# Rest tokens of a fused attention and expert kernel copied out of PSUM at once, and its first microseconds put in another order

## The chip, the cores and the metric

The kernel runs on one core of a Trainium2 chip. The core has a tensor engine (PE, with its weight loads shown as PEld), a vector engine (DVE), a scalar engine (ACT), GpSimd (POOL) and a sync engine (SP), which here only starts transfers. Each engine works through its own list of instructions in order; what one needs of another is told by semaphores. PE writes to PSUM, from which DVE and ACT read; everything else lies in SBUF. The metric is the device time of one execution in microseconds.

## The reference

The inputs are q, k and v of 8 batches, 8 heads, 576 positions and 64 columns, a table of 32 distance buckets by 8 heads, 4608 token numbers, and two weight tables of 8 experts (512x1024 and 1024x512).

```python
scores = (1 / sqrt(64)) * q @ k.T + bias_table[bucket(|i - j|)]
attn   = exp(scores - max) / (sum + 1e-9)
x      = (attn @ v) as 4608 tokens x 512
expert = token_ids * 2654435761 % 8
out[e] = max(x[e] @ w1[e], 0) @ w2[e]      # for each expert's tokens
```

## The kernel before, in words

Attention runs over 32 head pairs: pair n is batch n // 4 and heads 2m and 2m + 1 with m = n % 4. A pair has five score groups g. Groups 0 to 3 take 128 keys each against 512 queries of both heads; group 4 takes what is left over, since 576 is 512 and 64: the 64 "rest" tokens, as keys and as queries. The list `order` names all (n, g) and is worked through two at a time. For each two, PE makes the scores and the bias (products with a table `btb`, or for some groups a factor `ebd` that DVE multiplies in at L550), ACT takes the exponential of a group from PSUM into `att` (L540), then the functions `early` and `behind` add other work: transposes of later pairs, casts, and nine at a time the products of `att` with the values (`px`, L608) of a pair that is some groups back. DVE takes the reciprocal of the sums (L617) and writes the normalised output `x_all` (L618). PSUM has three slots for score groups and two others (aux 0 and aux 1). The output of a pair takes two tiles in turn, one in each of the two.

The order in each engine's list is the order in which the code writes the instructions (`manual_schedule`); nothing is reordered.

Loads: `load(j)` fetches q, k or v of the pairs 2j and 2j + 1 in two DMAs of 256 KB, or half of them with `h0, h1`; `load_rest(b)` fetches the rest tokens of batch b in eight small ones (q, k: L222; v: L234). Nearly all of them are issued by SP, in the order written. An issue takes one of eight semaphores in turn (DMAHW0 to 7 in the rows of the order), and waits until the transfer that used it before has landed. `load(3, "qk")` and `load(2, "v")` are the first ones issued from the loop, right behind the written list of the ramp. `cast_qk`, `cast_v` and `cast_vrest` make 16-bit copies: on POOL, for pairs 4 and up the values on DVE (L254), and for batches 1 and up the upper half of the rest values too (L277).

The bias table is made on the chip: one product (`bps`, L698), a copy by ACT (`ebsb`), a DMA to memory (`t_f`, L706) and from there DMAs that spread it over 128 partitions: `btb` (L712) for heads 0, 1, then 2 and 3, and so on, and the small `btr` (L725).

Rest tokens of a batch, `transpose_rest`: four products turn q and k of the rest tokens round into one PSUM slot (`pr`, L426); three DVE copies take them out, two into `kzr` (L434) and one into `qtr` (L443), and the slot is free after the third. It is called at (m, g) = (3, 0) of the batch before, after the nine `px` products of that step. The rest values go to `vt` in two halves of 64 partitions.

After the last pair the expert stage begins, at about 195 us of the span; it isn't touched.

Of the kernel before, what the change touches and what calls it, by code (L numbers as in the profile page):

```python
# [11 lines left out]
F32 = mybir.dt.float32  # L12
F16 = mybir.dt.float16
# [18 lines left out]
def kernel(  # L32
# [11 lines left out]
    nc = tc.nc  # L44

    B, H, S, D = q.shape
# [6 lines left out]
    P = 128  # L53
# [114 lines left out]
    with tc.tile_pool(name="at", bufs=1) as at, tc.tile_pool(  # L168
# [18 lines left out]
        btb = at.tile([P, H, 3, WB], F16, name="btb")  # L187
        btr = at.tile([P, NPAIR, GL + D + RU], F16, name="btr")
# [9 lines left out]
        qr, kr, vr = {}, {}, {}  # L198
# [17 lines left out]
        def load_rest(b, which="qkv", eng=None):  # L216
            for key, dst, src in (("q", qr, q), ("k", kr, k)):
                if key not in which:
                    continue
                dst[b] = at.tile([P, 2, 2 * D], F32, name=key + "r", bufs=2)  # L220
# [8 lines left out]
            if "v" in which:  # L229
                vr[b] = at.tile([P, NPAIR, D], F32, name="vr", bufs=2)  # L230
                for hh in range(2):
                    for c in range(2):
                        r0 = D * hh + RU * c
                        (eng or nc.sync).dma_start(  # L234
                            out=vr[b][r0 : r0 + RU, :, :],
# [37 lines left out]
        def cast_vrest(b):  # L273
            for hh in range(2):
                r0 = D * hh
                eng = nc.vector if b and hh else nc.gpsimd
                eng.tensor_copy(  # L277
                    out=vt[b % 2][r0 : r0 + D, :, VW * hh : VW * hh + D],
                    in_=vr[b][r0 : r0 + D, :, :],
                )  # L280
# [139 lines left out]
        def transpose_rest(b):  # L420
# [3 lines left out]
            for i, key in enumerate("kq"):  # L424
                for c in range(2):
# [6 lines left out]
                    )  # L432
            for hh in range(2):
# [5 lines left out]
                    in_=pr[D * hh : D * hh + D, 0, :, :].rearrange(  # L439
# [7 lines left out]
                in_=pr[:, 1, :, :].rearrange(  # L447
# [229 lines left out]
        guard.__enter__()  # L677
        load(0, "k", None, 0, 2)
        warm = at.tile([1, 1], F32, name="warm")
        nc.vector.memset(warm[:, :], 0.0)  # L680
        nc.scalar.activation(
# [12 lines left out]
        load(0, "v", None, 0, 2)  # L694

        cast_qk(0, nc.vector, nc.vector)
        bps = slot("bps")
# [24 lines left out]
        for hh in range(2):  # L722
            for c in range(2):
# [7 lines left out]
                )  # L731
        transpose_qk(0)
        for i in range(2):
# [14 lines left out]
        cast_v(0)  # L748
        load(1, "qk")
        load_rest(0, "v")  # L750
        load(0, "v", None, 2)
        load_band(2, 4, nc.sync)
# [6 lines left out]
        load_band(4, 6, nc.sync)  # L759
        load(2, "qk")  # L760
        load_band(6, H, nc.sync)
        load_rest(1)
# [86 lines left out]
        def behind(n, g):  # L849
            G = NIT * n + g  # L850
            b, m = pairs[n]
            if 5 <= n < 11 and g % 2 == 0:
                next(routing, None)
# [8 lines left out]
            if (m, g) == (3, 0) and b + 1 < B:  # L862
                transpose_rest(b + 1)
# [13 lines left out]
        def early(n, g):  # L877
# [5 lines left out]
            if (n, g) == (1, 0):  # L883
                rest_rest(0)
# [3 lines left out]
        order = [(n, g) for n in range(NP) for g in range(NIT)]  # L888
# [301 lines left out]
```

## Time and profile before

| | |
|---|---|
| median of 3 runs | 352.72 us (351.97 to 354.49) |
| the profiled execution's own time | 349.79 us |
| its span | 348.0 us |
| PE busy | 311.5 us, 90% |
| ACT busy | 204.3 us, 59% |
| DVE busy | 167.4 us, 48% |
| POOL busy | 149.6 us, 43% |

The span is what the trace covers; the own time has 1.79 us around it. Shares are of the whole span: ACT works almost without a break until the expert stage and little in it, so its share there says nothing of the attention stage. The views that split this by stage are among the rows below. In a timeline, a row that stands for several instructions gives the time from the first one's start to the last one's end.

### The profile page before, as it was taken

To read this page: it belongs to the slowest core of one execution; us is meant where nothing else is said; L and a number is where in the kernel's file an instruction comes from. 1 tells how busy PE (TensorE), PEld (TensorE's weight loads), DVE (VectorE), ACT (ScalarE), POOL (GpSimd) and SP (SyncE) were. 2 spreads that over 40 slices of the span, in tenths; PEclk is the share of its full clock that TensorE was granted. 3 is DMA by queue.
4 is the path that set the end of the run, shared out by engine and by line. 5 is a ranking of instruction groups with operands and counts; after the bars stand their busy time and mean duration, and the time that the engine had idled before them with its cause. 6 is when DMAs were issued, how large, how long until landed. Compare 5 with 4: busy or idle time off the path is not lost.

```text
span 348.0 us, 8924 instructions
## 1 busy us (share of the span) xinstructions
PE 311.5 (90%) x3688; PEld 198.8 (57%) x3688; DVE 167.4 (48%) x401; ACT 204.3 (59%) x239; POOL 149.6 (43%) x195
## 2 busy tenths in 40 slices
PE   3669898989999999998889899999999999999980
PEld 1245566666656666665647456665656656565640
DVE  2218589786686777768564313322223141405040
ACT  2579898899998999898885132242332414050600
POOL 6044232285657577655631514433425251514140
PEclk9999999999999999999999999999999999999996
DMA  5997929597989897889693295999998989982021
GB/s 168 255 280 226 279 53 289 167 314 223 288 238 272 268 281 208 229 192 146 119 221 91 76 329 208 188 212 245 282 221 220 155 218 137 227 136 110 24 106 48
DMA packets 90786, 69.15 MB, mean 199 GB/s; under 512 B 11975, under 2 KB 82407, under 8 KB 90736
## 3 DMA queue, kind: packets, MB, share of 16 engines
q0 software_dynamic: 17664, 30.96, 41.3%
q1 hardware_dynamic: 72416, 37.16, 38.4%
q8 instruction: 31, 0.51, 0.6%
q10 hardware_dynamic: 656, 0.36, 0.4%
q14 instruction: 19, 0.16, 0.1%
HBM read 69.47 MB, written 17.35 MB: 249 GB/s over the span
## 4 chain that ended last, share of the span: by engine, by line
PE 72%; DVE 9%; DMA 9%; ACT 4%; issue 2%; SPq 1%; POOL 1%; POOLq 0%; ACTq 0%; DVEq 0%
PE ops L1022 20%; PE hps L971 15%; PE px L608 10%; PE ps L498 8%; PE ps L475 6%; PE pqk L411 4%; PE hps L991 4%; ACT att L540 3%; DMA kf<-in_k_dram 3%; DMA btb<-t_f 3%; PE xps L948 2%; DVE att L550 2%; DMA vf<-in_v_dram 2%; PE ps L532 2%; PE hps L793 1%
## 5 line engine op out<-in xcount | busy, mean ns | idle before, releaser
L540 ACT ACTIVATE att<-ps 128x1024 f16<-128x1024 f32 x160 | 152.3, 1039 | 22.0 <-PE ps L498 14.9
L1027 DVE COPY ok<-ops 128x512 f32<-128x512 f32 (+1 forms) x41 | 27.8, 679 | 103.5 <-PE ops L1022 100.8
L1022 PE MATMUL ops<-w2t,h 128*128 128x512 f16 (+1 forms) x328 | 75.2, 374 | 2.2 <-PE px L608 1.7
L977 ACT ACTIVATE h<-hps 128x640 f16<-128x640 f32 x48 | 33.8, 704 | 71.9 <-PE hps L971 70.1
L1030 POOL DMA_INDIRECT out_dram<-ok,ids x40 | 39.6, 990 | 64.1 <-DVE ok L1027 53.9
L608 PEld LDWEIGHTS <-att 128*128 128x128 f16 x1408 | 55.6, 97 | 18.7 <-issue 13.4
L608 PE MATMUL px<-va,att 128*128 128x65 f16 x1280 | 59.3, 193 | 3.6 <-DVE kq L417 2.4
L971 PE MATMUL hps<-xpt,w1t 128*128 128x320 f16 x384 | 53.3, 299 | 0.5 <-DVE xpt L953 0.5
L498 PE MATMUL ps<-kq 64*128 64x512 f16 x256 | 46.2, 389 | 7.7 <-ACT att L540 6.0
L633 POOL DMA_INDIRECT t_xperm<-x_all,ds x40 | 40.5, 1012 | 24.7 <-DVE x_all L618 16.1
L475 PE MATMUL ps<-btb,idents 128*128 128x384 f16 (+1 forms) x256 | 45.8, 264 | 5.2 <-DMA btb<-t_f 5.0
L1022 PEld LDWEIGHTS <-h 128*128 128x128 f16 x328 | 30.8, 98 | 32.5 <-PE px L608 1.8
L971 PEld LDWEIGHTS <-w1t 128*128 128x128 f16 x384 | 37.5, 98 | 16.0 <-issue 0.7
L246 POOL CAST qh<-qf 128x512 f16<-128x512 f32 x31 | 19.4, 625 | 62.0 <-PE pqk L411 32.4
L550 DVE TENSOR_TENSOR att<-att,ebd 128x768 f16<-128x768 f16 x64 | 37.1, 581 | 6.4 <-ACT ebd L573 6.4
L417 DVE COPY kq<-pqk 128x1024 f16<-128x1024 f16 x32 | 22.1, 690 | 35.2 <-PE pqk L411 26.6
L498 PEld LDWEIGHTS <-kq 64*128 64x128 f16 x512 | 16.9, 94 | 33.6 <-issue 25.6
L618 DVE TENSOR_TENSOR x_all<-px,rcp 128x384 f16<-128x384 f32 x64 | 31.4, 491 | 2.2
L475 PEld LDWEIGHTS <-idents 128*128 128x128 f16 x336 | 20.6, 98 | 17.7 <-issue 12.9
L246 POOL CAST kh<-kf 128x512 f16<-128x512 f32 x31 | 26.9, 868 | 7.4 <-DMA kf<-in_k_dram 7.4
L999 ACT ACTIVATE h<-hps 128x768 f16<-128x768 f32 (+1 forms) x8 | 7.3, 918 | 23.9 <-DMA xpn<-t_xperm 8.9
L142 POOL DMA_DIRECT2D w1t<-in_moe_w_dram x8 | 6.5, 818 | 28.5 <-PE hps L971 25.1
(90 smaller groups left out, 288.9 us busy)
## 6 DMA issues: line engine op xcount, KB each, us to landing
w1t<-in_moe_w_dram POOLq DMA_DIRECT2D x8, 1024.0 KB
w2t<-in_moe_w_dram POOLq DMA_DIRECT2D x8, 1024.0 KB
qf<-in_q_dram SPq DMA_DIRECT2D x30, 256.0 KB
kf<-in_k_dram SPq DMA_DIRECT2D x30, 256.0 KB
vf<-in_v_dram SPq DMA_DIRECT2D x30, 256.0 KB
xpn<-t_xperm SPq DMA_DIRECT2D x6, 642.5 KB
t_xperm<-zx SPq DMA_DIRECT2D x8, 192.8 KB
btb<-t_f SPq DMA_DIRECT2D x3, 384.0 KB
```

The lines of the kernel that those rows point to most:

```text
L246: (eng or nc.gpsimd).tensor_copy(out=dst[n][:, :, :, :].transpose([0, 2, 1, 3]), in_=src[n // 2][:, 2 * (n % 2) : 2 * (n % 2) + 2].rearran ...
L475: nc.tensor.matmul(out=out, lhsT=idents[:, which, :], rhs=rhs, start=start, stop=True, skip_group_check=True,)
L498: nc.tensor.matmul(out=ps[:, hh, o : o + rhs.shape[1]], lhsT=lhsT, rhs=rhs, start=not biased and (g < KT or t == 0), stop=True, skip_group ...
L540: nc.scalar.activation(out=att[:, g, :, :], in_=ps[:, :, :], func=AF.Exp, bias=0.0, scale=scale,)
L550: nc.vector.tensor_tensor(out=a, in0=a, in1=ebd[:, 2 * m : 2 * m + 2, 1 - c : 3 - c, :], op=ALU.mult,)
L608: nc.tensor.matmul(out=po, lhsT=lhsT, rhs=rhs, start=(i == 0), stop=(i == len(todo) - 1), skip_group_check=True,)
L618: nc.vector.tensor_tensor(out=x_all[:, b % NRING, its[0] : its[0] + ni, :DM].rearrange("p t (m h d) -> p t m h d", h=2, m=NPAIR)[:, :, m, ...
L633: sc_in = nc.gpsimd.indirect_dma_start(out=xperm_d.ap()[:, :], out_offset=bass.IndirectOffsetOnAxis(ap=ds2[:, NIT * b + t : NIT * b + t + ...
L971: nc.tensor.matmul(out=hps[:, nr, : n // 2], lhsT=w[:, kt, ts(ft, P)], rhs=xt[i][:, kt, ts(nr, n // 2)], start=(kt == 0), stop=(kt == NPT ...
L977: nc.scalar.activation(out=hs[i][:, ft, :].rearrange("p (r n) -> p r n", r=2), in_=hps[:, :, : n // 2], func=AF.Relu, bias=0.0, scale=1.0,)
L1022: nc.tensor.matmul(out=ops[:, :w], lhsT=hs[i][:, ft, ts(sc, P)], rhs=w2t[e % 2][:, ft, d0 : d0 + w], start=(ft == 0), stop=(ft == NFT - 1),)
L1030: so = nc.gpsimd.indirect_dma_start(out=out[:, :], out_offset=bass.IndirectOffsetOnAxis(ap=ids[i][:, sc, :], axis=0), in_=ok[:, :], in_off ...
```

## The change

Four things are changed.

1. The rest tokens leave PSUM by one DVE copy of 128x512 into a tile `prs`; the three copies to `kzr` and `qtr` read that. `transpose_rest` of the next batch stands at (m, g) = (2, 4), ahead of that step's `px` products.
2. The rest values of both heads lie in one tile `vrz` with 128 partitions, zeros in the half that isn't a head's own, and one POOL copy takes them to `vt`. There is one such tile, and one each of `qr` and `kr`, instead of two.
3. In the ramp, groups (1, 0) and (1, 1) run before (0, 2) to (0, 4), and the scores of the rest tokens against each other (`rest_rest`) move to (1, 2). The bias tables of heads 2 to 5 are asked for earlier, ahead of value loads; the loads of q and k for pairs 2 to 5 are cut into halves of 128 KB. The first value load of pair 0 and 1 follows the bias tables.
4. 27 products with a zero operand (the tile `cnt`, cleared by DVE) run on PE ahead of the bias product, behind it and behind the first transposes. Nothing reads their result.

```diff
--- before.py
+++ after.py
@@ -185,6 +185,7 @@
         rr = [at.tile([P, (NPAIR + 1) * RC], F16, name=f"rr{i}")
               for i in range(2)]
         btb = at.tile([P, H, 3, WB], F16, name="btb")
+        vrz = at.tile([P, NPAIR, 2, D], F32, name="vrz")
         btr = at.tile([P, NPAIR, GL + D + RU], F16, name="btr")
         bro = [
             btr[:, :, GL * o : GL * o + D + RU] for o in range(2)
@@ -195,7 +196,7 @@
 
         pairs = [(b, m) for b in range(B) for m in range(NPAIR)]
         qf, kf, vf, qh, kh = {}, {}, {}, {}, {}
-        qr, kr, vr = {}, {}, {}
+        qr, kr = {}, {}
 
         def load(j, which="qkv", eng=None, h0=0, h1=4):
             for key, dst, src in (("q", qf, q), ("k", kf, k), ("v", vf, v)):
@@ -217,7 +218,7 @@
             for key, dst, src in (("q", qr, q), ("k", kr, k)):
                 if key not in which:
                     continue
-                dst[b] = at.tile([P, 2, 2 * D], F32, name=key + "r", bufs=2)
+                dst[b] = at.tile([P, 2, 2 * D], F32, name=key + "r", bufs=1)
                 for hh in range(2):
                     (eng or nc.sync).dma_start(
                         out=dst[b][:, hh, :],
@@ -227,12 +228,11 @@
                         ),
                     )
             if "v" in which:
-                vr[b] = at.tile([P, NPAIR, D], F32, name="vr", bufs=2)
                 for hh in range(2):
                     for c in range(2):
                         r0 = D * hh + RU * c
                         (eng or nc.sync).dma_start(
-                            out=vr[b][r0 : r0 + RU, :, :],
+                            out=vrz[r0 : r0 + RU, :, hh, :],
                             in_=bass.AP(
                                 v.tensor, ((b * H + hh) * S + NB4 + c) * D,
                                 [[2 * D, RU], [2 * S * D, NPAIR], [1, D]],
@@ -271,13 +271,12 @@
                 )
 
         def cast_vrest(b):
-            for hh in range(2):
-                r0 = D * hh
-                eng = nc.vector if b and hh else nc.gpsimd
-                eng.tensor_copy(
-                    out=vt[b % 2][r0 : r0 + D, :, VW * hh : VW * hh + D],
-                    in_=vr[b][r0 : r0 + D, :, :],
-                )
+            nc.gpsimd.tensor_copy(
+                out=vt[b % 2][:, :, :].rearrange(
+                    "p m (h d) -> p m h d", h=2
+                )[:, :, :, :D],
+                in_=vrz[:, :, :, :],
+            )
 
         def route_load():
             tid32 = moe_token_ids.bitcast(I32)
@@ -430,13 +429,15 @@
                         ),
                         identity=ident[:, :],
                     )
+            prs = at.tile([P, 2, 2, P], F16, name="prs")
+            nc.vector.tensor_copy(out=prs[:, :, :, :], in_=pr)
             for hh in range(2):
                 nc.vector.tensor_copy(
                     out=kzr[b % 2][D * hh : D * hh + D, :,
                                    D * hh : D * hh + D].rearrange(
                         "p m (c u) -> p c m u", c=2
                     ),
-                    in_=pr[D * hh : D * hh + D, 0, :, :].rearrange(
+                    in_=prs[D * hh : D * hh + D, 0, :, :].rearrange(
                         "p c (u m) -> p c m u", m=NPAIR
                     ),
                 )
@@ -444,7 +445,7 @@
                 out=qtr[b % 2][:, :, :].rearrange(
                     "p m (c u) -> p c m u", c=2
                 ),
-                in_=pr[:, 1, :, :].rearrange(
+                in_=prs[:, 1, :, :].rearrange(
                     "p c (u m) -> p c m u", m=NPAIR
                 ),
             )
@@ -675,9 +676,23 @@
             E_ALL.PE, E_ALL.Activation, E_ALL.Pool, E_ALL.SP, E_ALL.DVE,
         })
         guard.__enter__()
+        idle = aux(0, [P, 512], F32, "idle")
+
+        def idle_products(count):
+            for _ in range(count):
+                nc.tensor.matmul(
+                    out=idle[:, : 2 * P], lhsT=cnt[:, :P], rhs=cnt[:, :],
+                    start=True, stop=True, skip_group_check=True,
+                )
+
         load(0, "k", None, 0, 2)
         warm = at.tile([1, 1], F32, name="warm")
+        nc.vector.memset(cnt[:, :], 0.0)
         nc.vector.memset(warm[:, :], 0.0)
+        for hh in range(2):
+            nc.vector.memset(
+                vrz[D * hh : D * hh + D, :, 1 - hh, :], 0.0
+            )
         nc.scalar.activation(
             out=warm[:, :], in_=warm[:, :], func=AF.Exp, bias=0.0, scale=1.0,
         )
@@ -691,9 +706,9 @@
         load(0, "q", None, 0, 2)
         load(0, "qk", None, 2)
         load_rest(0, "kq")
-        load(0, "v", None, 0, 2)
 
         cast_qk(0, nc.vector, nc.vector)
+        idle_products(14)
         bps = slot("bps")
         nc.tensor.matmul(
             out=bps[:H, 0, : 3 * GN], lhsT=tbl[:, :], rhs=ohsb[:, :],
@@ -729,7 +744,9 @@
                         [[1, RU], [6 * GL, NPAIR], [1, GL + D + RU]],
                     ),
                 )
+        idle_products(8)
         transpose_qk(0)
+        idle_products(5)
         for i in range(2):
             nc.gpsimd.memset(kzr[i][:, :, :].bitcast(I32), 0)
             nc.gpsimd.memset(vt[i][:, :, :].bitcast(I32), 0)
@@ -745,20 +762,23 @@
         nc.gpsimd.memset(zx[:, :, :DM], 0.0)
         nc.gpsimd.memset(zx[:, :, DM:XW].bitcast(I32), NOID)
         cast_qk(1)
-        cast_v(0)
-        load(1, "qk")
+        load_band(2, 4, nc.sync)
+        load(0, "v", None, 0, 2)
+        load(1, "qk", None, 0, 2)
         load_rest(0, "v")
         load(0, "v", None, 2)
-        load_band(2, 4, nc.sync)
+        load_band(4, 6, nc.sync)
+        load(1, "qk", None, 2)
+        cast_v(0)
         cast_qk(2)
         cast_vrest(0)
         keep = at.tile([P, E, NGT], F32, name="keep", tag="ohk", bufs=1)
         nc.gpsimd.memset(keep[:, :, :], 1.0)
         nc.gpsimd.memset(keep[:, :, 0:1], 0.0)
         load(1, "v")
-        load_band(4, 6, nc.sync)
-        load(2, "qk")
         load_band(6, H, nc.sync)
+        load(2, "qk", None, 0, 2)
+        load(2, "qk", None, 2)
         load_rest(1)
 
         def fill_table(e):
@@ -849,6 +869,8 @@
         def behind(n, g):
             G = NIT * n + g
             b, m = pairs[n]
+            if (m, g) == (2, 4) and b + 1 < B:
+                transpose_rest(b + 1)
             if 5 <= n < 11 and g % 2 == 0:
                 next(routing, None)
             if G >= NIT + 2:
@@ -859,8 +881,6 @@
                 transpose_qk(n + 2)
             if n == NP - 1 and g in (2, 3):
                 head_transpose(g - 2)
-            if (m, g) == (3, 0) and b + 1 < B:
-                transpose_rest(b + 1)
             if g == 2 and n + 1 < NP:
                 cast_v(n + 1)
             if (m, g) == (2, 2) and b + 1 < B:
@@ -880,12 +900,13 @@
                 cast_rest(0, nc.vector)
                 transpose_qk(n + 1)
                 transpose_rest(0)
-            if (n, g) == (1, 0):
+            if (n, g) == (1, 2):
                 rest_rest(0)
             if (m, g) == (3, 3) and b + 1 < B:
                 rest_rest(b + 1)
 
         order = [(n, g) for n in range(NP) for g in range(NIT)]
+        order[2:7] = order[5:7] + order[2:5]
         for i in range(0, len(order), 2):
             both = order[i : i + 2]
             late = []
```

SP's list around the first bias tables (`btb`, `btr`). Before, from the last of the rest keys on:

```order
L222 DMA kr<-in_k_dram 128x1x128 [waits DMAHW6_49]
L208 DMA vf<-in_v_dram 128x2x128 [waits DMAHW7_49]
L208 DMA vf<-in_v_dram 128x2x128 [waits DMAHW0_49]
L712 DMA btb<-t_f 128x3x256 [waits DMAHW3_49,DMAHW1_49]
L725 DMA btr<-t_f 32x4x480 [waits DMAHW4_49]
L725 DMA btr<-t_f 32x4x480 [waits DMAHW5_49]
L725 DMA btr<-t_f 32x4x480 [waits DMAHW6_49]
L725 DMA btr<-t_f 32x4x480 [waits DMAHW7_49]
L208 DMA qf<-in_q_dram 128x4x128 [waits DMAHW0_49]
```

and now, from the same place:

```order
L223 DMA kr<-in_k_dram 128x1x128 [waits DMAHW6_49]
L727 DMA btb<-t_f 128x3x256 [waits DMAHW7_49,DMAHW1_49]
L740 DMA btr<-t_f 32x4x480 [waits DMAHW2_49]
L740 DMA btr<-t_f 32x4x480 [waits DMAHW3_49]
L740 DMA btr<-t_f 32x4x480 [waits DMAHW4_49]
L740 DMA btr<-t_f 32x4x480 [waits DMAHW5_49]
L727 DMA btb<-t_f 128x6x256 [waits DMAHW6_49]
L209 DMA vf<-in_v_dram 128x2x128
L209 DMA vf<-in_v_dram 128x2x128 [waits DMAHW0_49]
L209 DMA qf<-in_q_dram 128x2x128 [waits DMAHW1_49]
L209 DMA qf<-in_q_dram 128x2x128 [waits DMAHW2_49]
```

The two value loads of pairs 0 and 1 went behind the tables; the table of heads 2 and 3 (the `btb` with six rows) came forward to them; `qf` loads went from four heads to two.

ACT's list from the first exponentials on, before:

```order
L540 ACTIVATE att<-ps 128x1024 x4
L562 ACTIVATE ebd<-pf 128x2x384
L573 ACTIVATE ebd<-pg 128x2x192
L540 ACTIVATE att<-ps 128x1024 x2
L467 ACTIVATE rr_87<-prr 128x256
L540 ACTIVATE att<-ps 128x1024 x2
L562 ACTIVATE ebd<-pf 128x2x384
L573 ACTIVATE ebd<-pg 128x2x192
```

and now:

```order
L541 ACTIVATE att<-ps 128x1024 x6
L563 ACTIVATE ebd<-pf 128x2x384
L574 ACTIVATE ebd<-pg 128x2x192
L541 ACTIVATE att<-ps 128x1024 x2
L468 ACTIVATE rr_87<-prr 128x256
L563 ACTIVATE ebd<-pf 128x2x384
L574 ACTIVATE ebd<-pg 128x2x192
L541 ACTIVATE att<-ps 128x1024 x6
```

Six exponentials stand ahead of the first factors `ebd` where there were four, and the one of the rest tokens against the rest tokens (`rr`) stands between later groups.

DVE's list where batch 4 is prepared during the last pair of batch 3, before, from the kq copy of the pair's neighbour on:

```order
L417 COPY kq<-pqk 128x1024
L550 TENSOR_TENSOR att<-att,ebd 128x4x192
L277 CAST vt_81<-vr 64x4x64
L617 RECIPROCAL rcp<-px 128x6
L618 TENSOR_TENSOR x_all<-px,rcp 128x3x128
L550 TENSOR_TENSOR att<-att,ebd 128x4x192
L434 COPY kzr_83<-pr 64x2x4x32 x2
L443 COPY qtr_85<-pr 128x2x4x32
L617 RECIPROCAL rcp<-px 128x4
L618 TENSOR_TENSOR x_all<-px,rcp 128x2x128
```

and now, from the same copy:

```order
L416 COPY kq<-pqk 128x1024
L551 TENSOR_TENSOR att<-att,ebd 128x4x192
L433 COPY prs<-pr 128x512
L435 COPY kzr_83<-prs 64x2x4x32 x2
L444 COPY qtr_85<-prs 128x2x4x32
L618 RECIPROCAL rcp<-px 128x6
L619 TENSOR_TENSOR x_all<-px,rcp 128x3x128
L551 TENSOR_TENSOR att<-att,ebd 128x4x192
L618 RECIPROCAL rcp<-px 128x4
L619 TENSOR_TENSOR x_all<-px,rcp 128x2x128
```

The cast of `vt` is gone, the copies of the rest tokens went ahead of the reciprocal and the first `x_all`, and the copy `prs` stands ahead of them.

## Rows read from the trace of the kernel before

**Rows 1.** The page, busy time, share and instructions of the engines.
```profile
PE 311.5 (90%) x3688; PEld 198.8 (57%) x3688; DVE 167.4 (48%) x401; ACT 204.3 (59%) x239; POOL 149.6 (43%) x195
```

**Rows 2.** Windows by stage: length, busy time and count per engine, clock, DMA.
```profile
core 0: us, PE busy (x) PEld busy (x) DVE busy (x) ACT busy (x) POOL busy (x), PEclk, DMA share, GB/s
0.00:9.00 9.00, 3.70 (x17) 1.34 (x18) 1.81 (x5) 1.97 (x3) 5.23 (x22) 1.00 0.58 166
61.00:164.00 103.00, 96.78 (x1672) 65.61 (x1670) 77.61 (x196) 95.50 (x105) 62.86 (x77) 1.00 0.89 237
```

**Rows 3.** Chain of waits, 0 to 60 us: start, length, what.
```profile
7.00 1.74 DMA t_f<-ebsb
8.76 4.56 DMA btb<-t_f
...
33.16 5.66 DMA vf<-in_v_dram
```

**Rows 4.** Timeline of ACT in the ramp; in brackets the idle time ahead.
```profile
14.77 1.02 ACT L540 ACTIVATE att<-ps 128x1024 f16<-128x1024 f32 x1 [3.58 <-PE ps L498]
...
22.81 1.02 ACT L540 ACTIVATE att<-ps 128x1024 f16<-128x1024 f32 x1 [1.73 <-PE ps L475]
```

**Rows 5.** Timeline of SP in the ramp: its DMA issues.
```profile
7.62 1.11 SPq L208 DMA_DIRECT2D vf<-in_v_dram  x2
...
28.41 2.01 SPq L234 DMA_DIRECT2D vr<-in_v_dram  x4
```

**Rows 6.** Windows around the small rest loads; the last column is GB/s.
```profile
22.00:28.00 6.00, 5.69 (x92) 3.84 (x91) 2.39 (x5) 5.11 (x7) 1.39 (x3) 1.00 1.15 337
28.00:32.00 4.00, 3.86 (x61) 2.49 (x61) 2.86 (x7) 4.00 (x6) 2.92 (x5) 1.00 0.49 130
```

**Rows 7.** Timeline of DVE, the value cast that ends the ramp.
```profile
38.90 0.77 DVE L254 CAST va<-vf 128x512 f16<-128x512 f32 x1 [2.85 <-POOL qh L246]
```

**Rows 8.** Timeline of DVE at a batch boundary.
```profile
95.13 0.69 DVE L417 COPY kq<-pqk 128x1024 f16<-128x1024 f16 x1 [1.09 <-PE ps L498]
...
96.32 0.59 DVE L277 CAST vt<-vr 64x256 f16<-64x256 f32 x1
...
97.17 0.56 DVE L618 TENSOR_TENSOR x_all<-px,rcp 128x384 f16<-128x384 f32 x1
...
98.11 0.85 DVE L434 COPY kzr<-pr 64x256 f16<-64x256 f16 x2
```

**Rows 9.** Timeline of PE at the same boundary.
```profile
97.28 0.39 PE L498 MATMUL ps<-kq 64*128 64x512 f16 x2 [0.43 <-ACT att L540]
...
98.26 0.43 PE L608 MATMUL px<-va,att 128*128 128x65 f16 x9
```

**Rows 10.** Waits of PE, 53 to 165 us: total, times, longest.
```profile
PE ps L498 <- ACT att L540: 3.6, 9, 0.5
PE ps L498 <- DVE qtr L443: 1.1, 2, 0.6
```

**Rows 11.** Casts that bear on the copies: tile vr; DVE 53-165 us; POOL timeline.
```profile
L277 DVE CAST vt<-vr x7: 294/590/592, 32.7 to 158.8; 64x256 f16<-64x256 f32 x7
L266 DVE CAST krh<-kr 128x256 f16<-128x256 f32 x6 | 1.7, 282 | 0.0
95.78 0.98 POOL L246 CAST kh<-kf 128x512 f16<-128x512 f32 x1
```

**Rows 12.** Timeline of PE: bias product, and transposes early and late.
```profile
3.94 1.44 PE L698 MATMUL bps<-ohsb,tbl 32*8 32x387 f32 x2 [3.94 <-DMA ohsb<-t_bias_oh]
5.96 0.59 PE L411 MATMUL pqk<-idents,kh 128*128 128x128 f16 x4 [0.57 <-DMA idents<-t_ident]
...
22.88 0.38 PE L411 MATMUL pqk<-idents,kh 128*128 128x128 f16 x4
```

**Rows 13.** Rest values at that boundary: POOL cast, SP load of the next.
```profile
96.70 0.46 POOL L277 CAST vt<-vr 64x256 f16<-64x256 f32 x1
99.86 2.01 SPq L234 DMA_DIRECT2D vr<-in_v_dram  x4
```

## The prediction, made before the changed kernel was timed

> **What bounds the kernel now.** I read the page's busy shares first, then the windows by stage, the chain of waits over the ramp, the timelines of ACT, SP and DVE there, and last the places where one batch hands over to the next. TensorE (PE) is busy 90% of the span [rows 1]. The windows split this: PE has 3.70 us of work in the first 9, and 96.78 of 103 us from 61 to 164 [rows 2]. So the ramp has holes, and behind 61 us PE could give back 6.2 us at most. Nothing is edited behind 195 us.
>
> The ramp's holes hang on transfers. The chain [rows 3] reads: the bias vector out from 7.00 us, the first bias table back by 13.32, and later a value load, under way from 33.16 to 38.82. ScalarE (ACT) shows the table, and the one of the next heads, as waits of 3.58 and 1.73 us for score products [rows 4]; VectorE (DVE) shows the value load: it idled 2.85 us before its value cast at 38.90 [rows 7]. That third wait ends last, so the ramp's length is set there.
>
> The batch boundary is a small hole, repeated: PE waits 0.43 us for an exponential at 97.28 [rows 9]. From 53 to 165 us, which holds six boundaries, such waits, and those for the rest queries (qtr), sum to 3.6 and 1.1 us [rows 10].
>
> **Ramp.** Pair 1's first two groups now fill ACT's 3.58 us, and the table of heads 2 and 3 is asked for right behind the small rest tables, so the 1.73 us wait should go too. Both holes were inside the time that ends with the value load of pairs 4 and 5. I price the ramp by that load alone. In SP's queue, 34 issues stand between the rest keys of batch 0 and load 3 before, and 42 now; the value load comes four issues behind. Four small issues last 2.01 us together, 0.50 each [rows 5]. The eight more come from two loads cut in halves, so not one byte is added. If transfers set the pace, they cost 0; if SP's issuing does, 8 x 0.50 = 4.0 us. For transfers speaks that the queues moved 337 GB/s from 22 to 28 us; against it, that they fell to 130 from 28 to 32, when SP was handing out small rest loads [rows 6]. A half of 128 KB lasts 128/337 = 0.39 us at that rate, less than the 0.50 of its issue: sixteen halves lose 16 x 0.11 = 1.8 us if nothing is queued ahead. But from 22 to 28 us much is queued, because an issue waits only for the transfer eight before it, so I take 0.8 us of it. On the other side, the bias table no longer queues behind two value issues: 1.11 us [rows 5], of which I count half, 0.5. The net is 0.3 us slower. Ends: 1.1 us gained if the queue hides all halves, 4.0 us lost.
>
> The 27 zero products start when PE otherwise waits. Four transposing products of 128 columns last 0.59 us at 5.96 us and 0.38 at 22.88 [rows 12]. The granted clock stands at 1.00 in the first 9 us as later [rows 2], but the durations say that the first ran at the lower level (1.2 GHz) and the second at the upper (2.4). By the slower row, two 128-column pieces are at most 2 x 0.59/4 = 0.30 us, so 14 last at most 4.1 us; begun within the first microsecond, they end by 5.1, some 1.2 us after 3.94, where the bias product began [rows 12]. That product ends at 5.38 and the bias vector only leaves at 7.00 [rows 3], 1.6 us later: hidden. The other 13, 3.8 us by the same row and 2.5 by the faster, lie partly in waits of PE; I let them put back the first score products by up to some 1.5 us. What covers that is again the late value load; with that cover gone they would cost those 1.5 us. If they bring the upper clock earlier, the same cover hides the gain.
>
> The value cast of pair 1 now stands behind that of pair 4's q and k on GpSimd (POOL). This can hold the first output products of pair 1 for about a microsecond, inside DVE's 2.85 us of slack. The memsets of the zeroed halves are in DVE's idle first microseconds: 0.
>
> **Batch boundary.** DVE loses one cast of rest values, 0.59 us, and gains one copy out of PSUM. The three small copies stay; they now read SBUF and stand ahead of the first normalised output instead of behind it (DVE's order in the part on the change). The added copy has half the columns of the kq copy of 0.69 us: 0.35 [rows 8]. The small copies last 0.42 us from PSUM [rows 8]. No row shows them from SBUF. The nearest is the rest cast, 0.28 [rows 11]; bounds are 0.28 and the 0.59 that the value cast shows beside a POOL cast [rows 8, 11]. I take 0.31, near the first, which also has 256 columns and no POOL work on top of it. Then the first normalised output, which ends at 97.17 + 0.56 = 97.73 [rows 8], ends 0.35 + 3 x 0.31 - 0.59 = 0.69 later, at 98.42. PE's first output product of the next pair stood at 98.26; without the 0.43 us wait before it, it is ready at 97.83 [rows 9]. It now waits 0.6 us for that output, whose PSUM tile it overwrites. Behind it stand all of PE's score products, and behind them ACT.
>
> So 4.7/6 = 0.78 us of waits per boundary give way to about 0.6: a gain of 0.2 x 6 = 1.2 us. The seventh boundary lies in the ramp at 34 us, under the value load. With copies of 0.28 the new wait is 0.50 and the gain 1.7; with 0.42 it is 0.92 and 0.8 is lost; with 0.59 it is 1.43 and 3.9 is lost. PE's waiting disappears wholly at the other end: 4.7 gained.
>
> The small copies read from SBUF could be held up by POOL. Rows show such a thing: the value cast lasts 294 ns alone and 590 in the median, and just ahead of one of those, at 95.78, stands a POOL cast of 0.98 us [rows 8, 11]. The Trainium skill, "SBUF — State Buffer", section "Who interferes with whom", says that a DVE copy in a two-port mode and a POOL instruction lock each other out for the whole instruction, whoever comes first, and that this lock needs SBUF on both sides. This speaks against the change: copies from PSUM were outside it. By it the boundary would be the 0.59 end; I give this as a rival.
>
> **Single buffers.** Rest loads of the next batch now wait for casts out of the same tile. At the boundary near 97 us POOL's value cast starts at 96.70 and takes 0.46, while SP issues the first of those value loads at 99.86 [rows 13]. Spare: 2.7 us, cost 0. POOL's cast itself doubles in partitions only, and becomes one. Were the spare gone, load 3 and on would wait behind it on SP, some 0.5 us.
>
> **Sum.** 349.79 us is the profiled execution's own time (348.0 us of span and 1.79 around it). 349.79 + 0.3 - 1.2 = 348.9. It stood 2.93 us under the median of the runs, 352.72, so as a median I forecast 352.72 - 0.9 = **351.8 us**.
>
> **Rivals**, as medians. A measurement of this kernel tells about 1%, 3.5 us, from no change: faster is under 349.2, slower over 356.2.
>
> - *Forecast*, small gains that mostly cancel: 350.3 to 353.2, chance 0.50.
> - *Boundary waits vanish altogether.* For: the PSUM slot of the rest transposes comes free after one copy instead of three, and exponentials wait for slots. Against: DVE's added work sits straight ahead of an output that PE now waits for. 352.72 - 4.7 + 0.3 = 348.3; chance 0.20.
> - *Ramp gain survives.* If the value load is not the bound after all, DVE's 2.85 us come out too: 352.72 - 2.85 - 1.2 = 348.7. Against: the same bytes stand ahead of it. Chance 0.07.
> - *Slower: SP's issuing paces the ramp.* Eight more issues at 0.50 put the value load of pairs 4 and 5 back by 4.0 us, to about 42.8, and DVE's cast and PE's output products with it: 352.72 + 4.0 - 0.5 = 356.2 with less than half of the boundary gain. It decides once less than 4 us of transfers are queued when SP comes to the small rest loads; the fall to 130 GB/s speaks for it, 337 GB/s just ahead against. Chance 0.13.
> - *Slower: the port lock at the boundary.* Copies of 0.59 us: 352.72 + 3.9 + 0.3 = 356.9 if POOL holds all three, and about 354.4 if half. For: POOL's cast of 0.98 us stands at 95.78, just there [rows 11]. Against: one such cast covers one or two of the three copies. Chance 0.10.
>
> **Numbers.** Predicted 351.8 us. From 348.0 to 355.8 takes in the forecast, the two faster rivals nearly whole and the half-held lock, and leaves out the ends of both slower ones. Faster: the 0.20 and 0.07 lie at 348.3 and 348.7, near the line of 349.2, so 0.22 of 0.27. Slower: half of the 0.13 and a third of the 0.10, about 0.10. Within 1%: 0.68.
>
> **What would show it.** Ramp: ACT's waits of 3.58 and 1.73 us gone, DVE's wait before the value cast of pair 4 still there or longer, its load landing between 37.7 and 39.9 us. Boundary: PE's waits for the exponential and the rest queries replaced by one for the normalised output, 0.3 to 0.9 us each. Small copies at 0.28 to 0.42 us; at 0.59 the lock rival holds. Wrong would be a value load over 41 us or under 37, or boundaries with no wait on DVE at all.

## The result: slower, by the ramp and by the boundaries

The changed kernel takes 356.58 us (median of 9 runs, 355.22 to 359.04) beside 352.55 for the kernel before in the same rounds; ratio 1.0121, 95% interval 1.0093 to 1.0148: 4.0 us slower, where 0.9 us faster was forecast. The profiled execution took 355.22 us, its span 353.4 (before 349.79 and 348.0). The time lies just over the rival "SP's issuing paces the ramp" (356.2).

Two stages lost it, as the two traces show, whose spans lie 5.4 us apart (the medians 4.0). The first exponential of pair 8 starts at 64.71 us instead of 61.05, and that of pair 31 at 186.07 instead of 180.62: 3.7 us by the end of the ramp, and 1.8 more behind it, where the boundaries lie.

**The ramp after.** SP's timeline, with the same small rest loads and the value load of pairs 4 and 5 behind them [rows 5]:

```profile
23.46 0.63 SPq L727 DMA_DIRECT2D btb<-t_f  x1
24.14 1.54 SPq L209 DMA_DIRECT2D qf<-in_q_dram  x2
25.73 1.07 SPq L209 DMA_DIRECT2D kf<-in_k_dram  x2
26.84 0.98 SPq L209 DMA_DIRECT2D qf<-in_q_dram  x2
27.87 1.21 SPq L209 DMA_DIRECT2D kf<-in_k_dram  x2
...
32.02 1.96 SPq L234 DMA_DIRECT2D vrz<-in_v_dram  x4
34.02 1.89 SPq L209 DMA_DIRECT2D qf<-in_q_dram  x2
35.95 1.06 SPq L209 DMA_DIRECT2D kf<-in_k_dram  x2
37.05 1.19 SPq L209 DMA_DIRECT2D vf<-in_v_dram  x2
```

Read the starts: most halves take SP about 0.5 us, two a microsecond, with next to nothing between them. From 20 us until the value load SP waits 1.7 us in all; the rest is issuing. The value load goes out at 37.05 instead of 32.61. DVE's timeline shows its cast [rows 7]:

```profile
42.81 0.74 DVE L254 CAST va<-vf 128x512 f16<-128x512 f32 x1 [4.38 <-DMA vf<-in_v_dram]
```

42.81 against 38.90: 3.9 us late, with 4.38 us of waiting ahead. The rival had named 42.8. The holes that the change was to fill are partly gone: ACT's timeline [rows 4] shows 0.49 us where 3.58 stood, but a new wait later:

```profile
14.35 1.94 ACT L541 ACTIVATE att<-ps 128x1024 f16<-128x1024 f32 x2 [0.49 <-PE ps L499]
...
28.63 1.94 ACT L541 ACTIVATE att<-ps 128x1024 f16<-128x1024 f32 x2 [4.69 <-PE ps L499]
```

What stood behind it is in PE's timeline and in the windows (length, busy time of PE, PEld, DVE, ACT, POOL, granted clock, DMA share, GB/s):

```profile
22.41 0.44 PE L609 MATMUL px<-va,att 128*128 128x65 f16 x9
26.36 0.61 PE L410 MATMUL pqk<-idents,kh 128*128 128x128 f16 x4 [3.51 <-POOL kh L246]
...
27.98 1.03 PE L499 MATMUL ps<-kq 64*128 64x512 f16 x4
```

```profile
22.00:26.00 4.00, 0.85 (x22) 0.70 (x17) 0.00 (x0) 1.94 (x3) 0.92 (x2) 0.96 0.97 261
26.00:32.00 6.00, 5.64 (x46) 3.04 (x47) 2.89 (x7) 2.49 (x3) 2.26 (x5) 0.50 1.00 292
```

PE stood 3.51 us for POOL's cast of pair 3's k, and behind that idle time the granted clock reads 0.50 until about 32 us, the lower level (1.2 GHz): four score products last 1.03 us, 0.61 at the upper. This k is a second half, and it is late by its place as well: SP issued it at 21.38 us, behind the rest values, a value load and the table of heads 4 and 5; before, the k of pairs 2 and 3 went out whole at 13.33. Before, the same stretch had a clock of 1.00 and PE busy throughout. The DMA queues of the changed kernel moved 70 GB/s from 32 to 36 us, the hole that rows 6 showed at 28 to 32, now four microseconds later.

**The zero products.** PE's timeline of the first microseconds [rows 12]:

```profile
1.05 3.17 PE L683 MATMUL idle<-cnt 128*128 128x256 f16 x14 [1.05 <-DVE warm L691]
4.64 1.44 PE L713 MATMUL bps<-ohsb,tbl 32*8 32x387 f32 x2 [0.42 <-DMA ohsb<-t_bias_oh]
6.02 1.89 PE L683 MATMUL idle<-cnt 128*128 128x256 f16 x8
7.70 0.63 PE L410 MATMUL pqk<-idents,kh 128*128 128x128 f16 x4
```

Fourteen last 3.17 us and end at 4.22. The bias product starts 0.70 us later than before, but behind 0.42 us of idle time for its table `ohsb`: that transfer held it, not the products. The eight behind it put the first transposes at 7.70 instead of 5.96, and these still last 0.63 us as at the lower level.

**The boundaries after.** DVE's and PE's timelines at the boundary of rows 8 and 9:

```profile
100.19 0.42 DVE L433 COPY prs<-pr 128x512 f16<-128x512 f16 x1
100.64 0.91 DVE L435 COPY kzr<-prs 64x256 f16<-64x256 f16 x2
101.57 0.32 DVE L444 COPY qtr<-prs 128x256 f16<-128x256 f16 x1
101.81 0.18 DVE L618 RECIPROCAL rcp<-px 128x6 f32<-128x6 f32 x1
102.03 0.56 DVE L619 TENSOR_TENSOR x_all<-px,rcp 128x384 f16<-128x384 f32 x1
```

```profile
102.65 0.44 PE L609 MATMUL px<-va,att 128*128 128x65 f16 x9 [0.84 <-issue]
```

The order is as forecast: copies first, the normalised output behind. It ends at 102.59, and PE's product starts at 102.65 after 0.84 us of idle time, which the profile puts down to "issue" though the output had just ended. The two copies into `kzr` last 0.29 and 0.61 us here, where 0.31 was forecast for each; what stands beside the long one is read below, under the port lock.

### The profile page after: what moved, and what is told of

The parts are those of the page before. It is cut to its first block, busy times and chain, and to the rows that moved or that the text cites. A ratio compares the mean times of both kernels' runs of the same rounds, so it can differ in the third digit from the quotient of the medians.

```text
span 353.4 us, 8993 instructions
## 1 busy us (share of the span) xinstructions
PE 316.4 (90%) x3715; PEld 203.4 (58%) x3715; DVE 167.3 (47%) x405; ACT 203.9 (58%) x239; POOL 151.7 (43%) x194
## 4 chain that ended last, share of the span: by engine, by line
PE 73%; DVE 7%; DMA 6%; ACT 5%; SPq 3%; issue 2%; POOL 0%; POOLq 0%; ACTq 0%; DVEq 0%
PE ops L1043 19%; PE hps L992 15%; PE px L609 11%; PE ps L499 9%; PE ps L476 7%; ACT att L541 4%; PE pqk L410 4%; PE hps L1012 3%; DMA vf<-in_v_dram 3%; SPq L209 3%; PE xps L969 2%; DVE kq L416 2%; PE hps L813 1%; PE ps L533 1%; DMA btb<-t_f 1%
## 5 line engine op out<-in xcount | busy, mean ns | idle before, releaser
L609 PEld LDWEIGHTS <-att 128*128 128x128 f16 x1408 | 56.4, 98 | 22.8 <-issue 15.2
L609 PE MATMUL px<-va,att 128*128 128x65 f16 x1280 | 60.2, 194 | 9.1 <-DVE kq L416 3.6
L499 PE MATMUL ps<-kq 64*128 64x512 f16 x256 | 45.2, 389 | 5.3 <-ACT att L541 2.8
```

Of the source, the lines that this page charges most:

```text
L499: nc.tensor.matmul(out=ps[:, hh, o : o + rhs.shape[1]], lhsT=lhsT, rhs=rhs, start=not biased and (g < KT or t == 0), stop=True, skip_group ...
L609: nc.tensor.matmul(out=po, lhsT=lhsT, rhs=rhs, start=(i == 0), stop=(i == len(todo) - 1), skip_group_check=True,)
```

## The experiments

They ran on five chips (1, 9, 11, 12 and 15), on which the kernel before takes 344.2 to 345.0 us, not the 352.55 of the result. Each ratio is to the kernel before on the same chip in the same 5 rounds, with its 95% interval. The theories, by the names that the expectations use: SP's issuing makes the ramp late (1, later S); the order of SP's list does (2); the zero products do (3, later Z); POOL's list does, in which pair 1's value cast stands behind pair 4's q and k (P); and the boundaries lose by where the copies stand.

**The two kernels themselves, on chip 12.** No edit.

> The kernel before, unchanged, for its trace on the chip of the experiments and for the noise of a ratio: 1.000, within 0.003. If the experiments' ramps are late only because of the chip, DVE's value cast of pair 4 starts here at 40 to 41 us, not 38.90; if it starts at 38.9, each of them was late by what its change did.

> The changed kernel, unchanged, on the chip of the experiments: ratio 1.010 to 1.014 as at first if the loss doesn't depend on the chip; value cast of pair 4 some 3 to 4 us behind that of the kernel before beside it.

Ratios 1.0007 (0.9984 to 1.0030) and 1.0123 (1.0084 to 1.0162): the loss shows here too. The value cast of pair 4 starts at 40.14 and 42.85 us. DVE waits for it only 0.43 us here, before; PE's clock already reads 0.54 from 22 to 28 us. So single traces of the ramp differ without any edit: those below are set beside this one of the kernel before, mostly from another chip, and ratios carry the argument. PE's waits from 59 to 170 us (total, times, longest), before and after:

```profile
PE ps L498 <- ACT att L540: 2.6, 5, 0.5
PE ps L498 <- DVE qtr L443: 1.4, 4, 0.7
```

```profile
PE px L609 <- DVE x_all L619: 4.3, 6, 1.0
PE ps L499 <- DVE prs L433: 1.0, 2, 0.5
```

4.0 us of waits have turned into 5.3; counted from 62 us, so that both traces hold the same five boundaries, 3.3 have turned into 4.4. This is the boundary's loss in one view: from the first exponential of pair 8 to that of pair 31 the two kernels drift apart by 1.0 us. Unlike the ramp, this stretch repeats on these five chips: seven kernels with the transposes at their old place and three copies out of PSUM take 112.27 to 112.31 us for it, seven with the changed place 113.29 to 113.31. (Two others take more, by waits that are not all at boundaries: 113.34 us with zero products alone, where PE waits 1.3 us for a kq copy near pair 8, and 113.47 in one of the changed place.)

**Halves.** In the kernel before, halves alone (chip 9); in the changed kernel, whole loads again, where the first halves stood (chip 1).

```diff
-        load(1, "qk")
+        load(1, "qk", None, 0, 2)
+        load(1, "qk", None, 2)
```

(and `load(2, "qk")` alike).

> The kernel before with one thing changed: the loads of q and k for pairs 2 to 5 in halves, in their old place in SP's list. Theory S, eight issues more on SP put the value load of pairs 4 and 5 back: DVE's value cast of pair 4 between 41.4 and 42.8 us (38.90 before), ratio 1.007 to 1.011. Rival, the transfers set the pace and the halves are hidden: cast 38.5 to 39.5 us, ratio 0.998 to 1.002.

> The changed kernel with the loads of q and k for pairs 2 to 5 whole again (256 KB each, eight issues fewer on SP), placed where the first halves stood. Theory 1, SP's issuing sets the pace of the ramp: eight issues at 0.50 us come out, DVE's value cast of pair 4 starts near 38.9 us instead of 42.81, time 352.5 to 353.5 us, ratio to before about 1.003. Theory 2, the order of SP's list (tables ahead of values, nothing queued while the bias vector is on its way) costs the time and the halves are hidden: cast at 42 to 43 us, ratio about 1.011.

Alone 1.0052 (1.0030 to 1.0074), between what theory S and its rival named; taken back 1.0083 (1.0056 to 1.0111), whose interval still overlaps that of the whole change. SP's timelines of the halves and of the kernel before (chip 12):

```profile
35.73 1.21 SPq L208 DMA_DIRECT2D vf<-in_v_dram  x2
```

```profile
33.90 1.07 SPq L208 DMA_DIRECT2D vf<-in_v_dram  x2
```

The value load goes out 1.8 us later, and 0.52% of 344.2 is 1.8 us. The halves cost that much alone: theory S holds, at less than half of its 4.0. What became of the rest can be read from SP's own waits: 3.3 us from 9 us to the value load before, 1.5 with halves, so 1.8 of the 4.0 went where SP had waited for transfers. The cast moved from 40.14 to 42.69 in these two traces, the same way but further. The halves alone are some four tenths of the whole loss, and the only part of the change whose interval, alone, lies well clear of no change. No run has the changed kernel's own place for the second halves of pairs 2 and 3, behind the rest values, a value load and a table, without the other parts; the 3.51 us wait for pair 3's k may owe as much to that.

**Zero products.** Left out of the changed kernel (the three calls of `idle_products`), and put into the kernel before.

> The changed kernel without the 27 zero products. Theory 3, the zero products hold back the first kq copy (7.01 us before, 8.79 after) and all behind it follows: the value cast of pair 4 some 1.8 us sooner than 42.81, ratio about 1.007. Theories 1 and 2, the value load is late whatever PE does: cast at 42.5 to 43.1 us, ratio 1.010 to 1.014.

> The kernel before with the 27 zero products alone. Theory Z, they put back the first kq copy (7.01 us before, 8.79 in the changed kernel) and with it the first groups, and this is not covered: ratio 1.003 to 1.006. Rival, the value load of pairs 4 and 5 covers it: first kq copy late, value cast of pair 4 unmoved, ratio 0.998 to 1.002.

Left out 1.0077 (1.0041 to 1.0112), alone 1.0023 (0.9995 to 1.0051). With them left out the first kq copy comes at 7.43 us, yet the value cast is hardly sooner (42.21): theory 3's way isn't the one. Nor do they always delay that copy: on chip 12 it stands at 7.76 us in the changed kernel and at 7.71 before, where the first traces had 8.79 and 7.01. Neither interval parts the zero products clearly from no effect, so their size stays open.

**The order of SP's list, whole loads.** In the kernel before, `load_band(2, 4)` and `load_band(4, 6)` earlier, `load(0, "v", None, 0, 2)` and `cast_v(0)` behind them.

> The kernel before with SP's list in the changed order but whole loads: the tables of heads 2 to 5 earlier, the value loads of pairs 0 and 1 behind the first tables, POOL's first value cast behind them. If the order costs by itself (nothing is queued from 9 to 13 us while the bias vector is on its way, the first value cast waits until 17.5 us): ratio 1.002 to 1.006. If only the number of issues counts: ratio 0.997 to 1.002.

1.0010 (0.9989 to 1.0030): nothing. In a second kernel only the table of heads 2 and 3 came forward.

```diff
+        load_band(2, 4, nc.sync)
         load(1, "qk")
```

> The kernel before with one load moved: the table of heads 2 and 3 right behind the small rest tables, ahead of q and k of pairs 2 and 3. PE waited 2.0 to 2.4 us for it near 21 us, and its clock stood at the lower level behind that wait on this chip. If that wait counts: it goes, and the ratio is 0.993 to 0.998. If q and k, now later by a 384 KB transfer (1.1 us at 337 GB/s), take its place: ratio 0.999 to 1.003.

1.0026 (1.0003 to 1.0048): PE's wait for tables was shorter (4.5 us became 3.4), and 1.4 us for a normalised output and 1.1 for a cast of k came instead. Shortening the hole was worth nothing.

**Group order, and POOL's value cast of pair 1.** First the order alone in the kernel before (`order[2:7] = order[5:7] + order[2:5]`, and `rest_rest` with it); then the changed kernel without it; then the changed kernel with pair 1's value cast ahead, with half loads and with whole ones.

```diff
+            if n == 1:
+                cast_v(1)
             if n + 3 < NP:
                 cast_qk(n + 3)
```

(the old call for pair 1 goes).

> The kernel before with the group order alone: (1, 0) and (1, 1) run before (0, 2) to (0, 4). Theory P: on POOL the value cast of pair 1 now stands behind pair 4's q and k, which wait for their load; it starts near 29 us instead of 22.16, PE has no output products of pair 1 until then, ratio about 1.004. Theory S: only the value load of pairs 4 and 5 counts, its cast stays at 38.9 us and the ratio at 0.998 to 1.002.

> The changed kernel with the old order of the score groups, (0, 2) to (0, 4) ahead of pair 1. If the parts add up: 1.0123 less 0.002, ratio 1.008 to 1.012. If the group order makes the late loads hurt, since pair 1's value cast on POOL then stands behind pair 4's load and PE is idle near 28 us: ratio under 1.007.

> The changed kernel with POOL's value cast of pair 1 put ahead of pair 4's q and k casts, nothing else. Theory P: PE gets its output products of pair 1 some 5 us sooner and the ramp is shorter, ratio 1.004 to 1.008. Theory S: the value load of pairs 4 and 5 still lands at 42.7 us and ends the ramp, ratio 1.010 to 1.014.

> The changed kernel with both taken back: whole loads of q and k, and POOL's value cast of pair 1 ahead of pair 4's q and k. If S and P together are the loss in the ramp: value cast of pair 4 at 38.5 to 39.5 us, ratio 0.998 to 1.003. If the order of the tables and value loads or the zero products cost by themselves: cast at 40 us or later, ratio 1.004 to 1.008.

Alone 1.0019 (0.9991 to 1.0048); taken back 1.0135 (1.0095 to 1.0174); cast ahead 1.0167 (1.0131 to 1.0203), with whole loads 1.0066 (1.0036 to 1.0096). The cast of pair 1 did move, from 22 to 24 us in the kernel before to 31 in the changed one, and putting it ahead gained nothing clear of noise: with half loads PE then waits 4.04 us for the k cast of pair 3, with whole ones 2.36 for that of pair 4, and that cast is itself behind the load. Theory P fell as the cause, and so did the group order by itself.

**Do the parts add up?** The changed kernel without halves and without zero products.

> The changed kernel without the halves and without the zero products; the order of SP's list, the group order and the rest part stay. If the parts add up, 1.0123 less 0.004 for the halves and 0.0045 for the zero products: ratio 1.002 to 1.006. If the halves and the zero products cover each other's loss: still over 1.007.

1.0085 (1.0056 to 1.0114): they don't. PE's waits from 9 to 61 us, and windows:

```profile
PE px L609 <- POOL va L254: 5.2, 1, 5.2
PE pqk L410 <- POOL kh L246: 2.3, 1, 2.3
```

```profile
28.00:32.00 4.00, 0.00 (x0) 0.00 (x0) 0.34 (x1) 0.88 (x1) 1.37 (x3) 0.74 0.68 194
32.00:36.00 4.00, 3.48 (x37) 2.82 (x36) 1.07 (x3) 1.19 (x2) 2.76 (x5) 0.50 0.75 202
```

Here PE has no work at all for four microseconds, waiting for a value cast that stands behind the q and k of pair 4, and then runs at a granted clock of 0.50. Alone, the parts (halves, zero products, group order, order of the list, and the rest part below) sum to 0.52 + 0.23 + 0.19 + 0.10 + 0.16 = 1.20%, near the whole loss, though only the first of these is clear of zero; but taken back, halves and zero products leave PE another wait on late loads. That this is why they don't subtract is read from one trace, not shown by a run; the order of the list and the group order were never tried as a pair.

**Value load ahead.** In the kernel before, `load(2, "v")` ahead of `load_rest(1)`.

> The kernel before with the value load of pairs 4 and 5 moved ahead of the rest loads of batch 1 and the load of q and k for pairs 6 and 7 in SP's list: the same issues in another order. If this load ends the ramp, its cast starts 2 to 3 us sooner, without a wait of DVE for it, and the ratio is 0.992 to 0.996. If the rest loads, now later by two issues and 0.5 MB, hold DVE and PE instead: ratio 0.998 to 1.003.

0.9990 (0.9966 to 1.0013). The cast starts at 38.54 without a wait of DVE, and nothing is gained: the next kq copy waits 2.05 us for PE's transposes. On this chip, where DVE had waited only 0.43 us for it, the value load doesn't set the ramp's length. Whether it does where DVE waits 2.85 us, as in the first trace, no run shows.

**The rest part, the ramp part.** The kernel before with the rest part alone, and the changed kernel without it.

> The kernel before with the rest part alone: one tile vrz, single rest buffers, one copy out of PSUM, transposes at (2, 4); loads, zero products and group order as before. If the batch boundaries cost 1.6 us in all, as the starts of the exponentials in the two traces say: span about 349.6, ratio about 1.0045, value cast of pair 4 still at 38.9. If single buffers already hold back SP in the ramp: cast over 40 us and ratio over 1.008. If the boundaries cost nothing by themselves: ratio 0.998 to 1.002.

> The changed kernel with the rest part taken back: only the order of loads, the halves, the group order and the zero products differ from before. If the ramp holds 3.9 of the loss: value cast of pair 4 at 42.8 us, ratio about 1.009, and no further loss behind 61 us. If the parts need each other (rest loads that wait on the single buffers): cast nearer 39 us, ratio under 1.004.

1.0016 (0.9988 to 1.0043) and 1.0098 (1.0073 to 1.0123): the ramp part holds some 3.4 us of the loss. From pair 8 to pair 31 the first drifts by 1.0 us from the kernel before, the second not at all: the boundary's loss goes with the rest part.

**The place of the copies.** The copy `prs` alone, transposes at (3, 0) as before (the copy into `qtr` reads `prs` too); then the whole rest part with that place. The second differs from the rest part above in the place alone.

```diff
+            prs = at.tile([P, 2, 2, P], F16, name="prs")
+            nc.vector.tensor_copy(out=prs[:, :, :, :], in_=pr)
...
-                    in_=pr[D * hh : D * hh + D, 0, :, :].rearrange(
+                    in_=prs[D * hh : D * hh + D, 0, :, :].rearrange(
```

> The kernel before with the one copy out of PSUM alone: the rest transposes stay at (3, 0), behind the output products, and the three small copies read SBUF. If the loss at the boundaries (about 0.33 us each between the starts of exponentials) comes from the copies standing ahead of the first normalised output: no growth from pair 8 to pair 28 against the kernel before, or some gain, ratio 0.997 to 1.000. If it comes from the copies as such, four where there were three and beside POOL's casts: growth of 0.2 to 0.4 us a boundary, ratio 1.001 to 1.003.

> The kernel before with the rest part but for its place: one copy out of PSUM, one tile vrz, single rest buffers, transposes at (3, 0) behind the output products as before. If the place ahead of the output products is what costs at the boundaries: no waits of PE's output products for the normalised output, no growth against the kernel before from pair 8 to pair 28, ratio 0.995 to 0.999. If the single buffers or POOL's wider cast cost: ratio 1.001 or more with the place put right.

0.9968 (0.9946 to 0.9990) and 0.9945 (0.9917 to 0.9974): both beat both kernels, the second at 342.60 us beside 345.00. PE's waits from 59 to 170 us in it:

```profile
PE ps L499 <- ACT att L541: 2.5, 5, 0.5
```

The wait for the exponential is as before, that for the rest queries is gone, and none for the normalised output has come. From pair 8 to pair 31 it gains 1.2 us where the same part one step earlier lost 1.0. The place costs, not the copy, the single buffers or POOL's wider cast by themselves. But the place is two things: what the copies stand ahead of in DVE's list, and what POOL does beside them. Two boundaries of the changed kernel on chip 12, DVE's, POOL's and PE's timelines:

```profile
79.56 1.17 DVE L435 COPY kzr<-prs 64x256 f16<-64x256 f16 x2
79.36 0.60 POOL L246 CAST kh<-kf 128x512 f16<-128x512 f32 x1
79.91 0.67 POOL L274 CAST vt<-vrz 128x512 f16<-128x512 f32 x1
81.82 0.45 PE L609 MATMUL px<-va,att 128*128 128x65 f16 x9 [0.84 <-DVE x_all L619]
```

```profile
100.14 0.60 DVE L435 COPY kzr<-prs 64x256 f16<-64x256 f16 x2
99.52 1.12 POOL L634 DMA_INDIRECT t_xperm<-x_all,ds  x1 [0.17 <-issue]
100.16 0.39 PE L499 MATMUL ps<-kq 64*128 64x512 f16 x2 [0.50 <-DVE prs L433]
101.80 0.45 PE L609 MATMUL px<-va,att 128*128 128x65 f16 x9 [0.49 <-DVE x_all L619]
```

Beside POOL's casts the two copies take 1.17 us, beside its indirect DMA 0.60. From 57 us on, 5 of the 18 small copies of this trace last over 0.5 us, all beside such a cast; at the old place none does. At the three boundaries with held-up copies PE waits 0.84, 0.53 and 1.01 us for the normalised output, and the three copies take 0.61, 0.30 and 0.78 us longer than the 0.87 that they need alone. At the two others PE waits about 0.5 us for the copy `prs` and 0.5 for the output, 0.3 more than before, with no copy held up. So both work against the changed place; no run parts them.

## Why the prediction was wrong

**Ramp, +0.3 us: mis-sized, and the step that failed is "so I take 0.8 us of it".** Alone, the halves measure 1.8 us. The bounds of that sum reached to 4.0; the trace showed 4.4 us on the issue of the value load and 3.9 on its cast. I let queued transfers hide the halves, because an issue waits for the one eight before it. But eight halves in flight are half the bytes of eight whole loads: the queues moved 147 GB/s from 18 to 22 us (226 before). That this is why the issues showed is my reading; the order of the loads differs in that stretch too. The rival on SP's issuing had the place, and for the halves less than half of the price: that its 356.2 lies so near the measured 356.58 is partly luck, since the ramp part lost 3.4 us and only 1.8 of them are shown to be the halves. The other 1.6 stay open between the zero products, the two orders and the place of the second halves.

**Half a microsecond gained by the tables: not seen.** SP issued the first table at 9.08 us instead of 8.85, since the bias vector came no sooner.

**The cover.** "What covers that is again the late value load" isn't borne out: where the value load was taken away as a wait (the load ahead of the rest loads), nothing was gained, though only 0.43 us stood to be gained on that chip. The chain of waits named the end of one trace of the ramp; just under it stood others, the q and k of pair 4 and PE's clock behind idle time. Whether the zero products cost what the cover was to hide isn't settled (1.0023, from 0.9995); in the first trace they put the first score products from 7.76 to 9.54 us, 1.8 where up to 1.5 was allowed.

**Boundary, -1.2 us: wrong sign.** From pair 8 to pair 31 it lost 1.0 us on chip 12, and two steps failed. One is "I take 0.31, near the first, which also has 256 columns and no POOL work on top of it": the median small copy takes 0.29, but POOL's casts do stand beside some, and at the six boundaries behind the ramp a copy takes 0.38 us on average, in the first trace and in that of chip 12; `prs` takes 0.42 instead of 0.35. By the prediction's own sum that alone puts the output back by 0.42 + 3 x 0.38 - 0.59 = 0.97 us and makes PE's wait for it 0.87, more than the 0.78 that it replaces. The other is "without the 0.43 us wait before it, it is ready at 97.83". At two boundaries on chip 12 a wait stayed there: PE waits 0.50 us for `prs`, which holds the PSUM slot, where it waited for an exponential before, and then 0.49 for the normalised output on top.

**Port lock.** This rival was partly right. Some of the small copies, 5 of 18 from 57 us on, are held up, and by the prediction's own sign, copies at 0.59 us, those are the lock: 0.56 to 0.61 us in the first trace, 0.55 to 0.72 on chip 12. This adds 1.7 us to the 18 copies in either trace. That the same copies gain at the old place doesn't speak against it, since none is held up there. The Trainium skill, "SBUF — State Buffer", section "Who interferes with whom", has a DVE copy in a two-port mode and a POOL instruction shut each other out. The traces agree in that every copy over 0.5 us stands beside a POOL cast, though no run here shows the mode of a copy, and beside POOL's indirect DMA alone they take 0.28 to 0.34.

**Single buffers** cost nothing that shows, as forecast: they are in the fastest kernel of all.

## What to carry to other kernels

A load cut in halves doubles its price on the issuing queue (about 0.5 us an issue here, whole or half); where small loads stand ahead of the one that is waited for, compare the time of an issue with that of its transfer, and count the bytes in flight, not the transfers. Evacuating a PSUM slot in one copy pays (0.32% alone, at the old place), but not in front of the output that the tensor engine's next products overwrite, nor beside another engine's casts: ask who waits for the instruction that is pushed back, and what runs beside it at its new place; a median of copies hides the held-up ones. Where several waits end within a microsecond or two, taking one away shows the next, so a sum over one chain bounds the gain and doesn't forecast it.

## What the runs showed of the hardware that I had not expected

Behind 3.51 us of idle time PE's granted clock read 0.50 for some 6 us; before, in the first trace, the ramp held 1.00 behind a wait of 1.96 us, while the same kernel on chip 12 read 0.54 from 22 to 28 us, around a wait of 2.45. And 22 zero products just ahead did not bring the first transposes to the upper level in the changed kernel's first trace (0.63 us for four), while in its trace on chip 12, and in the kernel before with zero products alone, they lasted 0.38. What decided between them isn't settled; it isn't the kernel, since the same one did both.
